# Weights loaded by halves of their columns, and a new order of the list of pieces, in a kernel of segmented attention beside a dense layer

## The chip, the core and the metric

The program runs on one core of one Trainium2 chip. The metric is device time in microseconds (us) of one execution; the time before is the median of three executions. TensorE is called PE here (its weight loads PEld), VectorE DVE, ScalarE ACT, GpSimd POOL, SyncE SP. SP computes nothing: its queue issues DMAs, in order.

## What is computed

A layer norm of `x` (2,048 rows of 512) feeds two branches, and their outputs are added to `x`:

```python
xn  = _layernorm(x)
out = x + _A_ref(xn, wq, wk, wv, wo, beta) + _B_ref(xn, w1, w2)
# A: 32 heads of width 16, the rows in 4 segments of 512
for s in range(4):
    p = softmax(q_s k_s^T * scale + causal mask)
    o = g * (phi(q_s) M) / (phi(q_s) z + 1e-6) + (1 - g) * (p v_s)   # g = sigmoid(beta)
    M = M + phi(k_s)^T v_s ;  z = z + sum(phi(k_s))                  # phi(t) = t+1 if t>0 else exp(t)
A = o @ wo
# B: dense layer of width 1,792
B = silu(xn @ w1) @ w2
```

All inputs and the output are bf16.

## The kernel before

The program is one long list of short words, `ORDER`, run from left to right; each word calls one helper (the table `PIECES`) that issues a handful of instructions. No scheduler moves them afterwards: on each engine, and on each engine's queue of DMAs, the instructions stand in the order in which the words stand. An engine whose next instruction waits holds up everything behind it on that engine. A word is a name and numbers: most often the segment first, then the block.

- `X t.n`, `XD t`: transposing normalized rows into `xnT`, on PE with a copy (`Xa`, `Xv`; L717, L720) for row tiles 0 to 3, by a transposing DMA on SP (L726) for tiles 4 to 15. `xs`, `xq`/`xi`/`xg`, `Nv`: statistics, root and normalization of a tile (DVE L270/L271 and L293, POOL L275/L278).
- `k s.i.part`, `q`, `v`, `h`: the projections. A block fills one PSUM bank of 512 columns in two parts of two matmuls (segment 0 of k, q, h: two parts of four matmuls of 256 columns). L314 and L325.
- A letter behind it evicts the bank: `kv`, `qv`, `vv` on DVE, `ka`, `qa`, `va` on ACT (L340, L350, L357). An eviction of k is followed by a masked copy `kTo` on POOL (L341). For h, `ha` is a tanh on ACT (L438) and `hv` the product on DVE (L443).
- `S t`: scores of one batch, t = 20 times the segment + 5 times the block of 8 heads + batch. PE fills `psS`, four banks, of which there is one copy (L642); one exponential over 2,048 columns on ACT writes `Pb` (L649); POOL masks the diagonal (L657). The next `S` can't start on PE before this exponential has read `psS`. There are 80 of them.
- `E n`, `O n`: products of the weights with v, even and odd heads (16 small matmuls, L676), evicted by `Ev`/`Ea`, `Ov`/`Oa` (L699, L706), after which SP moves rows (L691, L710).
- `fp`, `fa`, `fv` and `gp`, `ga`, `gv`: phi of k and of q on POOL, ACT (L374) and DVE (L384). `t`: phi(k) transposed by a DMA (L392). `m`, `mv`, `mw`: the memory M. `s`, `sv`, `r`, `w`, `d`, `z`, `R`, `W`: the divisors, their reciprocals (L491, L506) and their spreading by DMAs (L523). `n`, `nv`: phi(q) M and its addition (L549, L556). `dv`, `zv`: products with the spread factors (L545, L535).
- `o s.j.i`: one of 18 matmuls of the output tile j (14 with w2, 4 with wo; L595); `oh`, `sh` the same for the last tile by halves of its columns. `xl` loads x again for the residual (L562), `st` evicts an output tile on DVE and stores it (L569, L574), `sh` half a tile (L613, L617).
- `lw0`, `lw1`: loads of w2 and wo, issued on ACT's queue. `busy` is idle work on PE at the start.

The projections, `E`, `O`, `n` and the output tiles j = 0, 1 of the last segment (all tiles of the others) share four PSUM banks, the pool `pp` (tag `pb`): a block that opens a bank waits until one of the four has been evicted.

The loads at the start are issued on SP in this order: x tile 0, x tile 2 (tiles 1 and 3 on ACT's queue), wv in two halves of its rows, wk, wq, x tiles 4 to 7 (`x_hi`), w1, x tiles 8 to 11, x tiles 12 to 15, beta. All of them share the core's 16 DMA engines.

Of the kernel before, what the change touches and what calls it, by code (L numbers as in the profile page):

```python
# [13 lines left out]


ORDER = """
ones0 ones1 zeros xs0 xs1 xq0 xi0 busy44 xq1 Nv0 xi1 X0.1 Nv1 Xa0.1 busy6 X1.1 Xa1.1 v0.0.0 xs2 xs3 xq2 v0.0.1 xq3 xi2 va0.0 v0.1.0 Nv2 v0.1.1 va0.1 xi3 X2.1 Nv3 odd tb Xv2.1 k0.0.0 X3.1 Xv3.1 q0.0.0 q0.0.1 qv0.0 k0.0.1 xs7 xs4 ka0.0 k0.2.0 xs6 fp0.0
S0 v0.3.0 k0.1.0 k0.2.1 fa0.0 xs5 xg4.4 v0.3.1 kv0.2
S2 q0.1.0 k0.1.1 q0.1.1 vv0.3 fp0.2 v0.2.0 kv0.1 fa0.2 Nv7 Nv4
S1 qv0.1 v0.2.1 h0.10.0 h0.10.1 h0.7.0 xs8 vv0.2 ha0.10 h0.7.1 hv0.10 ha0.7  # L20
S4 Nv5 h0.4.0 h0.4.1 ha0.4 h0.11.0 hv0.7 k0.3.0 h0.11.1 ha0.11 xs9 hv0.11 fv0.2
S7 k0.3.1 q0.3.0 XD4 q0.3.1 hv0.4 q0.2.0 XD5 XD7 q0.2.1 fa0.1
S6 qv0.3 qv0.2 h0.13.0 h0.13.1 t0.2 v1.3.0 ha0.13 v1.1.0
S3 v1.1.1 kv0.3 Nv6 xs11 h0.5.0 hv0.13 h0.5.1 xs10 ha0.5 xg8.4 XD6 E0 vv1.1
S5 v1.3.1 lw0 hv0.5 vv1.3 k1.0.0 xs14 k1.2.0 k1.2.1
S9 h0.1.0 Ev0 Nv10 kv1.2 Nv9 h0.1.1 k1.0.1 E1 ha0.1
S13 kv1.0 h1.11.0 XD10 h0.2.0 h0.2.1 ha0.2 h1.11.1 Ev1 fv0.0 hv0.1
S8 hv0.2 tanh O0 h0.8.0 h0.8.1 bmask Ov0 q1.1.0 ha0.8 hv0.8
S12 q1.1.1 q1.3.0 q1.3.1 fa0.3 fp0.1 kind qv1.1 O1
S10 k1.3.0 k1.3.1 Ov1 XD9 q1.2.0 qv1.3 fp0.3 ha1.11 q1.2.1 Nv8  # L30
S11 kv1.3 h0.0.0 v1.0.0 v1.0.1 h0.0.1 Nv11 ha0.0
S16 qv1.2 vv1.0 h0.12.0 h0.12.1 fv0.3 fa1.0 k1.1.0 k1.1.1 fp1.0 hv0.0
S14 E2 hv1.11 h1.9.0 kv1.1 h1.9.1 ha0.12 Ev2 hv0.12
S15 fv0.1 v1.2.0 h0.6.0 xs15 h0.9.0 h0.6.1 ha0.6
S17 v1.2.1 t0.0 ha1.9 hv0.6 h0.9.1 vv1.2 q1.0.0 t0.3 q1.0.1
S19 t0.1 m0.2 qv1.0 hv1.9 gp1.1 mv0.2 ha0.9 fv1.0 XD8 XD11 E3 O2
S18 h0.3.0 h0.3.1 Ev3 xl0.2 m0.0 hv0.9 k2.2.0 Ov2 xs13 ha0.3 hv0.3
# [60 lines left out]
"""


# [1 line left out]
def kernel(  # L102
# [692 lines left out]
```

## Time and profile before

| what | us |
|---|---|
| median of three executions | 231.76 (231.45 to 232.0) |
| the profiled execution, its time | 231.23 |
| its span, from the first to the last instruction | 229.5 |
| PE busy, share of the span | 221.5, 97% |
| ACT busy | 198.9, 87% |
| DVE busy | 171.8, 75% |
| POOL busy | 114.8, 50% |

The span is 1.7 us shorter than the time of the same execution, which also holds what lies around the program. The granted clock of TensorE was 1.000 over the span. Busy times of PE are modelled from the starts of its matmuls and include their pipelined ends, so a busy PE can still have short pauses; the starts themselves are what is read below.

### The profile page before, as it was taken

What the parts mean: (1) busy time and instruction counts of PE and PEld (TensorE: products, weight loads), DVE (VectorE), ACT (ScalarE), POOL (GpSimd) and SP (SyncE); (2) the same over time, 40 slices, a digit from 0 to 9 for tenths busy, and PEclk for the clock granted to TensorE, in tenths of its full rate; (3) what the DMA queues carried; (4) which work ended last, traced back from release to release, by engine and by line L of the source; (5) the groups of instructions that cost most, each with busy time, mean ns of one, the idle gap of its engine ahead of it and who ended that gap; (6) DMA issues with size and microseconds to landing.
All of it is one profiled execution on the core that took longest, in us unless ns stands there. A gap on an engine that the chain in (4) does not pass through costs nothing.

```text
span 229.5 us, 5243 instructions
## 1 busy us (share of the span) xinstructions
PE 221.5 (97%) x1984; PEld 103.6 (45%) x1984; DVE 171.8 (75%) x349; ACT 198.9 (87%) x179; POOL 114.8 (50%) x173
## 2 busy tenths in 40 slices
PE   7899999989999999999999999999999999999993
PEld 7657645445533433333433433344433443434552
DVE  4699997978978758866596967845796868874744
ACT  3789999999999999999999999999999999996000
POOL 6068557576474586564574474655444473332000
PEclk9999999999999999999999999999999999999999
DMA  6993256014302424241115232203032111132132
GB/s 200 366 371 70 57 169 195 18 31 74 73 17 54 140 72 101 59 94 30 33 38 98 75 83 76 64 9 98 25 96 81 52 32 58 32 88 83 34 116 94
DMA packets 34778, 20.40 MB, mean 89 GB/s; under 512 B 15680, under 2 KB 34240, under 8 KB 34752
## 3 DMA queue, kind: packets, MB, share of 16 engines
q1 hardware_dynamic: 32128, 17.45, 27.6%
q10 hardware_dynamic: 2624, 2.62, 3.7%
q8 instruction: 15, 0.25, 0.5%
q14 instruction: 11, 0.09, 0.1%
HBM read 9.96 MB, written 2.10 MB: 53 GB/s over the span
## 4 chain that ended last, share of the span: by engine, by line
PE 77%; ACT 13%; DMA 3%; issue 2%; DVE 1%; SPq 1%; DVEq 0%; ACTq 0%
PE ps L314 26%; PE psO L595 25%; PE psS L642 10%; ACT Pb L649 10%; PE psV L676 8%; DMA wq_sb<-in_A_wq_dram 3%; PE psS L595 3%; PE ps L325 3%; ACT th L438 2%; PE ps L549 1%; ACT ex L374 1%; PE psM L400 1%; SPq L176 1%; DVE hT L443 1%; DVE o_out L569 1%
## 5 line engine op out<-in xcount | busy, mean ns | idle before, releaser
L649 ACT ACTIVATE Pb<-psS 128x2048 bf16<-128x2048 f32 x80 | 150.2, 1878 | 5.2 <-PE psS L642 4.0
L657 POOL TENSOR_SCALAR_AFFINE_SELECT Pb<-Pb 128x512 bf16<-128x512 bf16 (+1 forms) x112 | 81.2, 739 | 82.2 <-ACT Pb L649 81.8
L595 PE MATMUL psO<-w_sb,hT 128*128 128x512 bf16 x196 | 60.2, 381 | 0.0
L443 DVE SCALAR_TENSOR_TENSOR hT<-th,ps 128x512 bf16<-128x512 bf16 x56 | 37.8, 681 | 21.1 <-ACT th L438 20.9
L314 PE MATMUL ps<-xnT,w_sb 128*128 128x512 bf16 x168 | 45.5, 380 | 0.0
L595 PEld LDWEIGHTS <-hT 128*128 128x128 bf16 x238 | 22.0, 98 | 26.7 <-issue 6.6
L438 ACT ACTIVATE th<-ps 128x512 bf16<-128x512 f32 x56 | 32.6, 595 | 0.4 <-PE ps L314 0.4
L314 PEld LDWEIGHTS <-w_sb 128*128 128x128 bf16 x168 | 15.2, 98 | 18.0 <-issue 3.1
L676 PE MATMUL psV<-Pb,Vz 128*32 128x128 bf16 (+3 forms) x512 | 22.2, 301 | 0.0
L642 PE MATMUL psS<-qT,kT 16*128 16x256 bf16 (+3 forms) x256 | 17.3, 301 | 1.3 <-ACT Pb L649 0.3
L595 PE MATMUL psO<-wo_sb,oT 128*128 128x512 bf16 x56 | 18.2, 380 | 0.0
L314 PE MATMUL ps<-wv_sb,xnT 128*128 128x512 bf16 x64 | 18.0, 381 | 0.1
L642 PE MATMUL psS<-qT,kTo 32*128 32x384 bf16 (+3 forms) x256 | 17.2, 299 | 0.8 <-ACT Pb L649 0.2
L676 PEld LDWEIGHTS <-Vz 128*32 128x32 bf16 x512 | 11.0, 96 | 13.4 <-issue 5.5
L341 POOL TENSOR_SCALAR kTo<-kT,pm_odd 128x512 bf16<-128x512 bf16 x16 | 11.9, 745 | 10.2 <-ACT kT L340 8.2
L325 PE MATMUL ps<-xnT,w_sb 128*128 128x256 bf16 x112 | 14.6, 273 | 0.0
L706 DVE CAST odd<-psV 128x512 bf16<-128x512 f32 x15 | 10.3, 686 | 4.9 <-PE psV L676 4.8
L314 PE MATMUL ps<-xnT,wk_sb 128*128 128x512 bf16 x48 | 13.3, 380 | 0.1
L350 DVE CAST qT<-ps 128x512 bf16<-128x512 f32 x16 | 10.8, 680 | 3.5 <-PE ps L314 2.2
L642 PEld LDWEIGHTS <-kT 16*128 16x128 bf16 x256 | 5.8, 91 | 16.7 <-issue 15.5
L314 PE MATMUL ps<-xnT,wq_sb 128*128 128x512 bf16 x48 | 12.8, 380 | 0.0
L325 PEld LDWEIGHTS <-w_sb 128*128 128x128 bf16 x112 | 10.4, 98 | 3.9 <-issue 1.5
(95 smaller groups left out, 258.0 us busy)
## 6 DMA issues: line engine op xcount, KB each, us to landing
spr<-rz SPq DMA_DIRECT2D x56, 64.0 KB
x_res<-in_A_x_dram SPq DMA_DIRECT2D x16, 128.0 KB
out_dram<-o_out SPq DMA_DIRECT2D x15, 128.0 KB
w_sb<-in_B_w_dram SPq DMA_DIRECT2D x1, 1792.0 KB
w_sb<-in_B_w_dram ACTq DMA_DIRECT2D x1, 1792.0 KB
x_hi<-in_A_x_dram SPq DMA_DIRECT2D x2, 512.0 KB
oraw<-odd SPq DMA_DIRECT2D x64, 16.0 KB
wv_sb<-in_A_wv_dram SPq DMA_DIRECT2D x2, 256.0 KB
```

What stands on the lines that cost most here:

```text
L314: nc.tensor.matmul(sts[s][key][:, :], lhsT=lhsT(ki), rhs=rhs(ki), start=(ki == 0), stop=(ki == DT - 1))
L325: nc.tensor.matmul(sts[s][name, i][:, cols], lhsT=w_sb[:, ki, i * P : (i + 1) * P], rhs=xnT[:, ki, cols], start=(ki == 0), stop=(ki == DT ...
L341: nc.gpsimd.tensor_scalar(out=kTo[:, dt, :], in0=kT[:, dt, :], scalar1=pm_odd[:, 0:1], scalar2=1.0, op0=ALU.mult, op1=ALU.mult,)
L350: copy(out=seg_tile(s, "qT")[:, dt, :], in_=sts[s].pop(("q", dt))[:, :])
L438: nc.scalar.activation(out=th[:], in_=sts[s]["h", ft][:, :], func=AF.Tanh, scale=0.5)
L443: nc.vector.scalar_tensor_tensor(out=st["hT"][:, ft, :], in0=st.pop(("th", ft))[:], scalar=1.0, in1=st.pop(("h", ft))[:, :], op0=ALU.add, ...
L595: mm = nc.tensor.matmul(st["psO", *key], lhsT=lhsT, rhs=rhs, start=len(done) == 1, stop=len(done) == FT + DT)
L642: nc.tensor.matmul(psS[:, g, c0 : c0 + nq], lhsT=kk[rows, dt, kt * P : (kt + 1) * P], rhs=st["qT"][rows, dt, kt * P : L], start=True, stop ...
L649: exp = nc.scalar.activation(out=Pb[:, :, :], in_=psS[:, :, :], func=AF.Exp, scale=SCALE)
L657: mask = nc.gpsimd.affine_select(out=blocks, in_=blocks, compare_op=ALU.is_ge, fill=0.0, base=0, pattern=[[0, blocks.shape[1]], [1, P]], c ...
L676: nc.tensor.matmul(psV[32 * g : 32 * g + 32, kt * P : L], lhsT=Vzs[s % 2][:, kt, 4 * dt + g, par : par + 2, :].rearrange("p a d -> p (a d) ...
L706: copy(out=odd[:], in_=sts[s].pop(("psV", 1))[:, :])
```

## The change

Two things change. First, wk, wq and w1 are each loaded by two DMAs, the first half of the columns of wk and wq before the second halves. A row of wk or wq is 1,024 B in memory and each DMA now takes 512 B of it; of w1 1,792 B instead of 3,584 B:

```diff
-    def load_w(eng, w_sb, W, k0, k1):
-        eng.dma_start(out=w_sb[:, k0:k1, :], in_=W.rearrange("(ko ki) n -> ki ko n", ki=P)[:, k0:k1, :])
+    def load_w(eng, w_sb, W, k0, k1, cols=slice(None)):
+        eng.dma_start(out=w_sb[:, k0:k1, cols], in_=W.rearrange("(ko ki) n -> ki ko n", ki=P)[:, k0:k1, cols])
 
     load_w(nc.sync, wv_sb, A_wv, 0, 2)
     load_w(nc.sync, wv_sb, A_wv, 2, 4)
-    load_w(nc.sync, wk_sb, A_wk, 0, 4)
-    load_w(nc.sync, wq_sb, A_wq, 0, 4)
+    for cols in (slice(0, D // 2), slice(D // 2, D)):
+        load_w(nc.sync, wk_sb, A_wk, 0, DT, cols)
+        load_w(nc.sync, wq_sb, A_wq, 0, DT, cols)
     load_x(nc.sync, 4, 4)
-    load_w(nc.sync, w1_sb, B_w1, 0, DT)
+    for cols in (slice(0, F // 2), slice(F // 2, F)):
+        load_w(nc.sync, w1_sb, B_w1, 0, DT, cols)
     load_x(nc.sync, 8, 4)
     load_x(nc.sync, 12, 4)
```

Second, `ORDER` is another order of the same 1,147 words, apart from seven evictions that change engine: `va0.2`, `qa3.2` and `Oa14` go from DVE to ACT, `vv3.3`, `kv3.0`, `Ev9` and `Ev15` from ACT to DVE. The new order came out of the same planning as the old one, with longer transposing transfers, last evictions and last stores assumed in it; the helpers are unchanged. Shown are its start and its last steps, and of the new list two steps between them:

```diff
-ones0 ones1 zeros xs0 xs1 xq0 xi0 busy44 xq1 Nv0 xi1 X0.1 Nv1 Xa0.1 busy6 X1.1 Xa1.1 v0.0.0 xs2 xs3 xq2 v0.0.1 xq3 xi2 va0.0 v0.1.0 Nv2 v0.1.1 va0.1 xi3 X2.1 Nv3 odd tb Xv2.1 k0.0.0 X3.1 Xv3.1 q0.0.0 q0.0.1 qv0.0 k0.0.1 xs7 xs4 ka0.0 k0.2.0 xs6 fp0.0
-S0 v0.3.0 k0.1.0 k0.2.1 fa0.0 xs5 xg4.4 v0.3.1 kv0.2
-S2 q0.1.0 k0.1.1 q0.1.1 vv0.3 fp0.2 v0.2.0 kv0.1 fa0.2 Nv7 Nv4
-S1 qv0.1 v0.2.1 h0.10.0 h0.10.1 h0.7.0 xs8 vv0.2 ha0.10 h0.7.1 hv0.10 ha0.7
-S4 Nv5 h0.4.0 h0.4.1 ha0.4 h0.11.0 hv0.7 k0.3.0 h0.11.1 ha0.11 xs9 hv0.11 fv0.2
-S7 k0.3.1 q0.3.0 XD4 q0.3.1 hv0.4 q0.2.0 XD5 XD7 q0.2.1 fa0.1
-S6 qv0.3 qv0.2 h0.13.0 h0.13.1 t0.2 v1.3.0 ha0.13 v1.1.0
-S3 v1.1.1 kv0.3 Nv6 xs11 h0.5.0 hv0.13 h0.5.1 xs10 ha0.5 xg8.4 XD6 E0 vv1.1
-S5 v1.3.1 lw0 hv0.5 vv1.3 k1.0.0 xs14 k1.2.0 k1.2.1
-S9 h0.1.0 Ev0 Nv10 kv1.2 Nv9 h0.1.1 k1.0.1 E1 ha0.1
-S13 kv1.0 h1.11.0 XD10 h0.2.0 h0.2.1 ha0.2 h1.11.1 Ev1 fv0.0 hv0.1
-S8 hv0.2 tanh O0 h0.8.0 h0.8.1 bmask Ov0 q1.1.0 ha0.8 hv0.8
-S12 q1.1.1 q1.3.0 q1.3.1 fa0.3 fp0.1 kind qv1.1 O1
-S10 k1.3.0 k1.3.1 Ov1 XD9 q1.2.0 qv1.3 fp0.3 ha1.11 q1.2.1 Nv8
...
-S79 w3 h3.13.0 h3.13.1 ha3.13 hv3.11 o2.1.15 xl2.1 o2.1.1 h3.6.0 h3.10.0 hv3.13 d3.3 o2.1.0
-S78 o2.1.14 h3.10.1 R0.3 h3.9.0 h3.6.1 R0.1 o2.1.13 d3.0 o2.1.11 R0.0 o2.1.6 R0.2 W0 ha3.10
-S76 o2.1.9 hv3.10 ha3.6 o2.1.3 d3.1 o2.1.8 h3.9.1 o3.1.0 o3.1.2 dv3.0 o3.1.13 ha3.9 dv3.3 o3.1.8 o3.1.4 oh3.1 oh12.1 o3.2.12 z3.2 z3.0 o3.1.11 o3.2.2 oh0.0 hv3.6 hv3.9 d3.2 o3.2.0 E15 Ea15 O15 o3.1.1 o3.2.13 zv3.0 o3.1.5 o3.2.3 Oa15 o2.1.10 dv3.2 o3.0.12 o3.0.5 o3.2.5 z3.1 xl3.1 n3.0 xl3.3 o3.0.6 nv3.0 zv3.2 o3.2.9 o3.0.0 o3.2.6 o3.0.4 o3.2.4 o2.1.12 n3.2 o2.1.5 oh2.0 oh14.1 oh2.1 oh12.0 o3.2.1 o3.2.14 dv3.1 oh6.1 oh5.1 nv3.2 o3.1.16 o3.0.11 o3.1.9 oh8.1 R1.1 o3.0.3 oh5.0 oh10.1 R1.3 oh6.0 oh10.0 o2.1.2 oh7.0 o3.0.10 oh13.1 o3.0.2 R1.0 oh9.0 R1.2 o3.1.12 n3.1 oh14.0 W1 z3.3 o3.2.10 o3.0.1 o3.2.11 o3.1.7 oh11.1 o3.2.7 o3.1.14 zv3.1 nv3.1 o3.0.9 o3.0.13 st2.1 o3.2.8 oh15.0 n3.3 zv3.3 oh16.0 oh8.0 oh3.0 o3.0.15 o3.0.14 o3.0.16 oh1.0 o3.0.7 o3.2.16 nv3.3 oh11.0 o3.2.17 o3.2.15 xl3.2 o3.1.6 o3.0.8 oh4.0 oh17.0 st3.2 o3.1.10 oh13.0 o3.0.17 o3.1.15 o3.1.17 o3.1.3 sh0 oh16.1 oh9.1 st3.0 oh4.1 st3.1 oh1.1 oh15.1 oh0.1 oh17.1 oh7.1 sh1
+ones0 ones1 zeros xs0 xs1 xq0 xi0 busy44 xq1 Nv0 xi1 X0.1 Nv1 Xa0.1 busy6 X1.1 Xa1.1 v0.0.0 xs2 xs3 xq2 v0.0.1 xq3 xi2 va0.0 v0.1.0 Nv2 v0.1.1 va0.1 xi3 X2.1 Nv3 odd tb Xv2.1 k0.0.0 X3.1 Xv3.1 q0.0.0 q0.0.1 qv0.0 k0.0.1 v0.2.0 xs6 xs4 k0.1.0 xs5 xs7 ka0.0 fa0.0
+S0 q0.1.0 k0.2.0 v0.2.1 xg4.4 va0.2 k0.2.1 fp0.0
+S2 k0.1.1 kv0.2 k0.3.0 k0.3.1 fa0.2 kv0.1 kv0.3 Nv5 q0.1.1
+S4 v0.3.0 XD5 v0.3.1 h0.7.0 h0.7.1 ha0.7 fv0.0
+S1 Nv7 qv0.1 h0.13.0 h0.13.1 Nv4 h0.11.0 Nv6 h0.11.1 hv0.7 fp0.2 ha0.13 fp0.1 vv0.3 q0.3.0 ha0.11 XD7
+S6 q0.3.1 h0.4.0 xs13 h0.4.1 tanh hv0.13 qv0.3 hv0.11 XD4 ha0.4 v1.3.0 xs9 xs11 hv0.4 h0.5.0 xs10
+S7 v1.3.1 h0.5.1 vv1.3 q0.2.0 fa0.1 XD6 q0.2.1
+S5 E0 qv0.2 ha0.5 Ev0 h0.10.0 xs8 h0.10.1 fv0.1 v1.1.0 ha0.10 hv0.10
+S16 v1.1.1 h0.1.0 h0.1.1 ha0.1 E1 vv1.1 fp0.3
+S3 q1.1.0 fv0.2 xg8.4 hv0.5 q1.1.1 h0.8.0 Ev1 h0.8.1 ha0.8
+S9 xs14 k1.2.0 k1.2.1 qv1.1 hv0.8 h0.2.0 fa0.3 t0.0 O0 t0.1
+S8 kind kv1.2 h0.2.1 k1.1.0 Ov0 ha0.2 k1.0.0 k1.0.1 Nv10 hv0.1 Nv11
+S14 hv0.2 XD10 h1.11.0 Nv8 k1.1.1 h1.11.1 ha1.11 Nv9 kv1.1 XD8 k1.3.0
+S11 XD11 k1.3.1 v1.0.0 kv1.0 lw0 kv1.3 hv1.11 v1.0.1 vv1.0 h0.12.0
+S12 O1 h0.9.0 h0.12.1 q1.0.0 Ov1 ha0.12
+S10 fp1.0 q1.3.0 fv0.3 h0.9.1 hv0.12 ha0.9 q1.0.1 h0.6.0 qv1.0 t0.3
+S15 v1.2.0 q1.3.1 h0.6.1 hv0.9 h0.3.0 ha0.6
+S13 qv1.3 E2 hv0.6 XD9 h0.3.1 t0.2 bmask h0.0.0 Ev2 ha0.3 v1.2.1
+S19 h0.0.1 gate ha0.0 vv1.2 k2.1.0 hv0.3 k2.1.1 O2
...
+S20 v2.1.0 xs12 v2.1.1 hv1.8 sv0 o0.0.0 o0.0.12 r0.3 vv2.1 xl0.2 h1.4.0 ha1.0 o0.0.3
+S23 h1.4.1 h1.10.0 r0.0 o0.0.13 h1.10.1 ha1.4 r0.2 o0.0.2 r0.1 o0.0.7 hv1.0 ha1.10 w0 z0.3 o0.0.5 gp1.3 z0.2 gp1.2 hv1.10
...
+S77 h3.10.1 st2.2 ha3.10 hv3.5 o2.1.11 h3.7.0 r3.0 w3 h3.6.0 h3.6.1 R0.2 hv3.10 R0.0 o2.1.15 o2.1.2 xl3.0 R0.3 o2.1.1 h3.7.1 ha3.6 hv3.6 o2.1.10 d3.0 o2.1.0 ha3.7
+S79 R0.1 o3.0.1 W0 o3.0.5 o3.0.10 d3.1 o2.1.17 o2.1.16 h3.11.0 o3.0.6 h3.11.1 o3.0.12 ha3.11 o3.0.3 hv3.7 o3.0.2 hv3.11 o2.1.9 dv3.1 o3.0.8 dv3.0 d3.2
+S78 z3.1 E15 h3.9.0 z3.0 o3.0.0 o2.1.7 h3.9.1 ha3.9 o2.1.12 z3.2 oh11.1 oh7.0 Ev15 dv3.2 oh1.0 oh7.1 o2.1.5 hv3.9 o3.2.1 o3.2.6 o2.1.3 O15 Oa15 zv3.1 o2.1.13 n3.1 o3.2.13 nv3.1 zv3.2 oh2.1 zv3.0 o3.2.7 n3.2 o3.2.8 o3.0.13 o3.0.11 o3.2.4 nv3.2 oh12.1 oh15.0 o3.0.9 o2.1.8 n3.0 R1.3 o3.1.5 nv3.0 o3.0.16 oh3.0 o3.1.7 o3.1.3 o3.1.8 R1.1 R1.0 d3.3 oh10.1 o3.2.16 o3.1.16 oh15.1 oh9.1 o3.2.9 oh4.0 o3.2.5 oh0.0 o3.2.3 oh4.1 R1.2 o3.2.15 o3.1.11 oh0.1 oh14.0 oh13.0 oh1.1 W1 oh16.0 z3.3 oh10.0 o3.1.13 o3.0.7 dv3.3 o3.0.14 o3.2.2 o3.1.1 o3.2.12 oh11.0 o3.2.11 oh13.1 oh6.0 oh12.0 oh2.0 o3.0.4 oh5.0 n3.3 o3.2.14 st2.1 zv3.3 oh8.1 o3.2.0 o3.1.14 oh3.1 nv3.3 o3.1.12 o3.0.15 o3.1.4 o3.0.17 o3.2.10 oh17.0 oh16.1 o3.2.17 o3.1.10 oh6.1 xl3.3 o3.1.2 o3.1.6 oh17.1 xl3.1 oh5.1 st3.0 oh14.1 oh8.0 oh9.0 st3.2 o3.1.15 sh0 sh1 o3.1.9 o3.1.0 o3.1.17 st3.1
```

In the words of the list, what changes by place: in front of S0 stand `v0.2.0`, `k0.1.0` and `fa0.0` in the new list and `k0.2.0` and `fp0.0` in the old one. The load of w2 (`lw0`) stands in the step of the 13th score batch (S11) instead of the 8th (S5). The last score batch is S78 instead of S76, with `E15` right behind it; the list ends with the store of a whole tile (`st3.1`) instead of half a tile (`sh1`).

## The prediction, made before the changed kernel had run

> **What bounds it now.** I read the page first, then the chain of waits in order of time, then the timeline of the start and of the end. Of the page:
>
> ```profile
> PE 221.5 (97%) x1984; PEld 103.6 (45%) x1984; DVE 171.8 (75%) x349; ACT 198.9 (87%) x179; POOL 114.8 (50%) x173
> ...
> PE   7899999989999999999999999999999999999993
> ...
> ACT  3789999999999999999999999999999999996000
> ```
>
> PE and ACT are both full from slice 3 on, and ACT runs out three slices before PE: the end is set by PE, its work plus its pauses. The chain gives the prices of PE's words:
>
> ```profile
> 203.09 0.33 PE psS L642 x4
> ...
> 205.03 0.65 PE psO L595 x3
> ```
>
> An S is 0.33, an output product 0.22, so a part of a projection (two such matmuls) 0.43; an E or O, in another line of the chain, 0.66. Now the timeline of the start:
>
> ```profile
> 10.25 0.77 PEld L325 LDWEIGHTS <-wq_sb 128*128 128x128 bf16 x8 [0.82 <-DMA wq_sb<-in_A_wq_dram]
> ...
> 11.77 0.59 ACT L340 CAST kT<-ps 128x512 bf16<-128x512 f32 x1 [0.91 <-PE ps L325]
> 11.95 0.69 DVE L270 BATCH_NORM_STATS2 stats<-x_hi 128x6 f32<-128x512 bf16 x1
> ...
> 12.41 0.39 PE L642 MATMUL psS<-qT,kT 16*128 16x512 bf16 x4 [0.24 <-ACT kT L340]
> ...
> 12.86 1.88 ACT L649 ACTIVATE Pb<-psS 128x2048 bf16<-128x2048 f32 x1 [0.50 <-PE psS L642]
> ...
> 15.24 1.88 ACT L649 ACTIVATE Pb<-psS 128x2048 bf16<-128x2048 f32 x1
> ...
> 17.61 1.88 ACT L649 ACTIVATE Pb<-psS 128x2048 bf16<-128x2048 f32 x1
> ...
> 20.38 1.87 ACT L649 ACTIVATE Pb<-psS 128x2048 bf16<-128x2048 f32 x1
> ```
>
> The reader is to see two things. From one exponential to the next are 2.38 us (12.86, 15.24): 1.88, then 0.50 until the next scores are there, in which one short activation fits; with two tanhs between them it is 2.77 (17.61, 20.38). And the row of 10.25 names what S0 hangs on, below. With the prices I add PE's words between two S and hold them against the starts of the S on PE (first at 12.41, last, S76, at 205.61: 79 steps in 193.20). A step takes the larger of 2.38 and its PE words plus 0.11 (steps of 2.48 take 2.59 or 2.60). Counted off the old list: 60 steps with up to 2.28 of PE words, 16 with 2.48 to 2.50, 3 with 2.70: 60 x 2.38 + 16 x 2.60 + 3 x 2.81 = 192.8, 0.4 under the measured time. So the old list ran nearly without waits that its words don't explain, and four terms make the span: 12.41 to S0; 193.20 of steps; from S76 to PE's end 20.39 (20.00 of words, 0.23 of waits, 0.16 for the last matmul to drain; end at 226.0); and the tail, 3.51.
>
> **The start, before S0.** PE waits for wq until 10.25, and the eviction of k, S0 and the first exponential hang on that. By the trace's landing events wk is complete at 8.35, wq at 10.21, x_hi at 11.69, w1 at 16.41, one after another: the loads are bound by the DMA engines. A packet of 1,024 B from memory takes 46 ns, one of 3,584 B 144; packets of 512 B appear only from on-chip memory (27 ns), those of 256 B take 18. I take 27. A half of wk is 32 packets on each of 16 engines, 32 x 27 = 0.86 us (bounds: 0.58 at 18, 1.47 at 46). The first halves of wk and wq then land 1.7 us behind wv (6.96), with the spread of the engines near 9.0 (8.1 to 9.9). The next limit is the copy of x tile 3, done at 10.06: `q0.0.0` follows `X3.1` at 9.44, `q0.0.1` starts at 10.17, then `k0.0.1` (to 11.05), `v0.2.0` and `k0.1.0` (to 11.92), while ACT evicts k from 11.25 to 11.84. S0 at 11.95: **-0.46** (0 if wq still came at 10.2). `v0.2.0` is 0.43 of PE work that S0 no longer has behind it; it shows in the last term. `fa0.0` falls into the 0.50 in which ACT waits for S0: free.
>
> **Behind the loads.** All packets of wk and wq cost 128 x 27 instead of 64 x 46 ns: x_hi at 11.69 + 0.51 = 12.20 (bounds: 11.05 at 18 ns, 14.63 at 46). w1 by 1,792 B, between 46 and 144 ns, 75 on the line through both: 64 x 75 against 32 x 144, +0.2, so w1 at about 17.1; its first reader `h0.7.0` comes near 18.0. Three more issues on SP of some 0.5 us, ahead of a transposing DMA that comes only at 18: free. But the four statistics of x_hi now head DVE's queue, and behind them stand `kv0.2`, `kv0.1`, `kv0.3`, whose PSUM banks PE wants back. At 0.80 a statistic and 0.60 an eviction (three in a row start at 15.15, 15.72 and 16.32 in the timeline) DVE is done with `kv0.2` at 16.05 (`v0.3.0` wants its bank at 17.1), `hv0.7` at 20.9 (`q0.3.0`: 21.2), `hv0.4` at 26.3 (E0: 27.05), `vv1.3` at 27.7 (`h0.10.0`: 27.7), `hv0.10` at 30.95 (E1: 30.8, but the S behind it can't start before 31.9). I take no stall; the cover is 0 to 1 us thick, and what DVE loses beyond it PE loses too.
>
> **The steps.** Counted off the new list: 68 steps up to 2.29, 8 with 2.48 to 2.50, and 2.71, 3.56, 3.78 once each: 68 x 2.38 + 8 x 2.60 + 2.82 + 3.67 + 3.89 = 193.0. The same 0.4 that the count missed before makes 193.4. Added: steps with two tanhs. In S5 PE has only 2.28: +0.39 less slack, 0.36; S23 (2.48), +0.16; S0 with `va0.2` (0.64 on ACT) +0.07, S7 +0.06. The other four doubles lie in or before longer PE steps: nothing. Sum **194.0** (193.4 without these).
>
> **Moved DMAs.** w2 is now loaded from about 42 to 49 us. The one transposing DMA under the old load of w2 (issued 34.47) landed after 4.0 us, others after 2.4 to 2.5. Under it or just behind now come `O1`'s row moves, `t0.3` and XD9 on SP: six issues of 0.5 to 0.6, two of 1.2, XD9 landing near 53.1; `k2.1.0` reads it at 54.1. Free by 1.0; with 1.5 us more it costs 0.5. The seven evictions that change engine are one more for DVE, one less for ACT, inside steps with room; free, else 0.6 once.
>
> **The end.** From S78 PE has 18.48 of words, against 20.00; with the same 0.39, **18.87**. The late chain there is `O15`, ACT's copy, the row moves (1.55 from issue to landing), the `R1`, the spread (2.1), `zv3.3`, `nv3.3`. Before, `nv3.3` ended 11.6 after O15 on PE and its first reader came 11.9 after it; now, with SP free of the first two row moves, I get 10.4 against a reader at 11.0. Free, by 0.6. The tail before:
>
> ```profile
> 226.11 0.41 DVE L613 SCALAR_TENSOR_TENSOR o_half<-psS,x_res 128x256 bf16<-128x256 f32 x1
> ...
> 227.06 0.40 SPq L617 DMA_DIRECT2D out_dram<-o_half  x1
> ```
>
> The half tile was evicted by 226.52, but SP was issuing other stores until 226.97; it landed 1.61 after its issue. Now a whole tile comes last: eviction to 0.8 after PE's end, SP free, landing 1.84 to 1.90: 2.7 in all, as before (2.67). Tail **3.5**.
>
> **Sum.** 11.95 + 194.0 + 18.87 + 3.5 = 228.3 against 229.5: -1.2. The profiled execution took 231.23, 0.53 under the median shown: 230.0 in its frame, **230.6** against the median of 231.76.
>
> **Rivals.**
> 1. *No room lost* (231.76 - 1.85 = 229.9): the doubled tanhs hide in slack that I don't see. For: the old S1, S4 and S77, each with two, cost nothing beyond PE's words. Against: S5 has few of these. 0.12.
> 2. *The halves don't bring wq earlier*, because one slow engine sets the landing (12 of 16 engines had wq by 9.2, the last at 10.21). S0 stays at 12.41: 230.6 + 0.46 = 231.0. 0.08.
> 3. *DVE's queue eats it*: each eviction counts its full 0.68 instead of 0.60. Fourteen of them stand up to `hv0.10`: 32.05 instead of 30.95, so E1 ends at 32.75 and S3 comes 0.85 late: 231.4. For: bank by bank the cover is thin. Against: three evictions in a row in the old run kept 0.60. Within 0.2%. 0.18.
> 4. *Slower: x_hi is late.* If a 512 B packet from memory costs what one of 1,024 B does, x_hi lands at 14.63 and all that DVE does until `Ev1` shifts by 2.4 us, PE with it by about 2.2: 232.8. It decides from a stall of about 1.2, x_hi at 13.5 (37 ns a packet). Against: 27 ns in this trace; for: not one of these came from memory. 0.15.
>
> The Trainium skill, page "DMA: Bandwidth & Descriptors", section "Bandwidth", speaks for rival 4: it wants DMAs batched to 1 MiB and gives 2.0 us plus the bytes at 436 GB/s for each. By that, an estimate, four loads of 256 KB one behind the other take 10.4 us instead of 6.4, and x_hi would be 4 us late. The trace disagrees so far: whole wk and wq landed 1.4 and 1.9 us behind their forerunners, so loads in one queue overlap their fixed parts.
>
> **Chances and range.** Forecast 0.47, rivals 0.12, 0.08, 0.18, 0.15. About 0.2% (0.46 us) can be told from no change: faster (under 231.3) is the forecast and rivals 1 and 2, 0.67; same rival 3, 0.18; slower rival 4, 0.15. The forecast's own range is 230.0 to 231.2, by the stalls taken as nothing and the double tanhs; the range of 8 in 10 goes down past rival 1 and up through rival 3 to the near part of rival 4: 229.5 to 232.4.
>
> **What would show it.** Right: no wait for wq at the first q, S0 at 11.9 to 12.0, x_hi's first statistic near 12.2, S78 near 206, O15's reader of `nv3.3` unstopped, a tail of 3.5. Wrong: a first statistic after 13, PE waiting for DVE's evictions between 17 and 33 us, a pause before `k2.1.0`, or steps of 2.27 that take more than 2.4.

## The result, and the profile after

| | median, us | range | runs |
|---|---|---|---|
| kernel before, same chip | 232.12 | 231.45 to 232.75 | 6 |
| changed kernel | 237.91 | 236.48 to 239.2 | 6 |

The ratio is 1.0254, with a 95% interval from 1.0213 to 1.0295: the changed kernel is slower by 2.5%, where 230.6 us and a small gain were forecast. The profiled execution took 237.82 us, its span 236.1, against 228.3 in the prediction's sum. Of the page after:

```profile
PE 223.9 (95%) x1984; PEld 103.6 (44%) x1984; DVE 173.7 (74%) x350; ACT 198.9 (84%) x178; POOL 114.7 (49%) x173
...
PE   7998999995999999999899999999999999999992
...
PEclk9999999999799999999999999999999999999999
```

The loss is local. PE's row has one slice at 5, the tenth (53 to 59 us), and the clock that PE was granted has one slice below 9, the eleventh. PE's work is the same, so a longer span means pauses. The start, by contrast, came out as forecast; in the timeline of the start:

```profile
11.81 0.69 DVE L272 BATCH_NORM_STATS2 stats<-x_hi 128x6 f32<-128x512 bf16 x1 [0.36 <-DMA x_hi<-in_A_x_dram]
...
11.95 0.39 PE L644 MATMUL psS<-qT,kT 16*128 16x512 bf16 x4
```

S0 starts at 11.95, and x_hi's first statistic at 11.81, 0.14 ahead of the old run. (Lines of the code stand two further down than before.) The waits of PE between 11 and 230 us are few. Before:

```profile
PE psS L642 <- ACT Pb L649: 0.6, 2, 0.3
PE psS L642 <- ACT kT L340: 0.2, 1, 0.2
```

and after (us in total, times, the longest):

```profile
PE ps L316 <- DMA xnT<-xn_t: 2.7, 1, 2.7
PE psM L402 <- DMA phiK<-pk: 0.9, 1, 0.9
PE ps L327 <- DMA xnT<-xn_t: 0.7, 1, 0.7
```

Three single waits replace the short ones for ACT. The longest, in the timeline of PE:

```profile
54.17 0.40 PE L644 MATMUL psS<-qT,kTo 32*128 32x384 bf16 x8
54.50 0.61 PE L327 MATMUL ps<-xnT,w_sb 128*128 128x256 bf16 x4
57.82 1.02 PE L316 MATMUL ps<-xnT,wk_sb 128*128 128x512 bf16 x4 [2.71 <-DMA xnT<-xn_t]
...
61.11 1.06 PE L402 MATMUL psM<-Vz,phiK 128*128 128x128 bf16 x8
```

The 57.82 row is `k2.1.0` in S19, which reads what XD9 transposes. Its cause lies 15 us earlier, in the timeline of SP's queue:

```profile
42.73 4.29 SPq L728 DMA_TRANSPOSE xnT<-xn_t  x3
47.12 1.14 SPq L693 DMA_DIRECT2D zraw<-odd  x2
48.31 4.66 SPq L712 DMA_DIRECT2D oraw<-odd  x4
53.08 2.05 SPq L394 DMA_TRANSPOSE phiK<-pk  x1
55.17 1.26 SPq L728 DMA_TRANSPOSE xnT<-xn_t  x1
```

The three transposes at 42.73 are XD10, XD8 and XD11. The load of w2 was issued on ACT's queue at 42.71. By the landing events it lasted until 52.4, and the three landed 6.8, 8.4 and 7.3 us after their issue, instead of 2.4 to 2.5. Nobody on PE waits for them yet; SP does. In the view of SP's waits between 40 and 60 us the fourth row move of O1 stands behind one of them:

```profile
SPq L712 <- DMA xnT<-xn_t: 2.3, 1, 2.3
```

That move left at 52.46, t0.3 at 53.08 (its issue alone took 2.05 us instead of 1.2), XD9 at 55.17 (my estimate was 50.7). The trace says why a row move waits for a transpose of other data. Each DMA of this program reports its landing on a semaphore, a counter; there are eight of them for all DMAs, on SP's queue and on ACT's, used nearly in turn, and in none of the twelve traces does a DMA leave before the one that used its semaphore last has landed. The move of 52.46 has the semaphore of XD8 (landed 52.45), t0.3 that of XD11 (52.98), and XD9 that of the load of w2 itself (52.44): XD9 could not have left before that, however fast the transposes. XD9 itself was quick, issued 55.17 and landed at 57.69: it was sent late, not carried slowly. And PE did not come back at full speed; the windows of the same stretch (busy time of each engine, granted clock, DMA share, GB/s):

```profile
56.00:58.00 2.00, 0.18 (x1) 0.13 (x2) 0.00 (x0) 0.99 (x2) 1.23 (x2) 1.00 0.45 92
...
59.00:60.00 1.00, 1.00 (x24) 0.42 (x16) 0.15 (x1) 0.00 (x0) 0.00 (x0) 0.53 0.02 4
60.00:61.00 1.00, 1.00 (x10) 0.28 (x3) 1.00 (x2) 0.60 (x1) 0.00 (x0) 0.50 0.55 131
61.00:62.00 1.00, 1.00 (x10) 0.89 (x9) 0.13 (x1) 1.00 (x1) 0.00 (x0) 0.50 0.01 2
62.00:63.00 1.00, 1.00 (x11) 0.61 (x10) 0.79 (x2) 0.80 (x2) 0.65 (x1) 0.77 0.03 6
```

The granted clock is 0.50 for 3.41 us after the pause: the eight matmuls of M at 61.11 take 1.06 instead of 0.61. (In two of the six executions, 236.48 and 237.87 us, the mean granted clock was 0.998 and 1.000, and such a stretch alone takes off 0.007: there it was missing.) Held against the prediction's rule (the larger of 2.38 and the PE words plus 0.11), the steps around it are too long by 3.18 (S19), 1.08 (S17) and 0.14 (S18): 4.4 us of the 7.8 by which the span was missed. The rest is in smaller pieces: S1 0.83, S42 1.12, S28 0.52, the last stretch 0.33, the tail 0.63.

S1, in the timeline of DVE:

```profile
17.16 1.58 DVE L386 SCALAR_TENSOR_TENSOR pk<-ex,pos 128x512 bf16<-128x512 bf16 x1
...
19.96 1.49 DVE L295 TENSOR_SCALAR xn_t<-x_hi,mv_all,rstd_all 128x512 bf16<-128x512 bf16 x2
21.37 0.67 DVE L445 SCALAR_TENSOR_TENSOR hT<-th,ps 128x512 bf16<-128x512 bf16 x1
```

`fv0.0` takes 1.58 and the two normalizations 1.49, where elsewhere such an instruction takes 0.68 and 0.40. So `hv0.7` (21.37) ends at 22.04 instead of the 20.9 that I had worked out, and `q0.3.0` starts at 22.09; the profile puts that wait down to a transposing DMA (XD7), which landed at 22.11, behind that start, and whose rows `q0.3.0` does not read. S42, in the chain of waits:

```profile
113.02 3.92 DMA phiK<-pk
```

`m1.0` waited for t1.1's transpose, which landed 3.92 us after its issue at 113.02. At 114.52 a load of instructions (16,384 B, 0.88 us) ran on the same DMA engines. The tail, in the timeline of DVE:

```profile
231.14 0.69 DVE L571 SCALAR_TENSOR_TENSOR o_out<-psS,x_res 128x512 bf16<-128x512 f32 x1 [1.26 <-PE psS L597]
...
232.41 0.68 DVE L571 SCALAR_TENSOR_TENSOR o_out<-psO,x_res 128x512 bf16<-128x512 f32 x1
```

PE ended at 231.96, but `st3.1`, the last eviction, stood behind `st3.2` and two half tiles and started at 232.41.

### The profile page after: what moved, and what is told of

Same layout as the page of the kernel before. It is cut to its first block, busy times and chain, and to the rows that moved or that the text cites. A ratio compares the mean times of both kernels' runs of the same rounds, so it can differ in the third digit from the quotient of the medians.

```text
span 236.1 us, 5232 instructions
## 1 busy us (share of the span) xinstructions
PE 223.9 (95%) x1984; PEld 103.6 (44%) x1984; DVE 173.7 (74%) x350; ACT 198.9 (84%) x178; POOL 114.7 (49%) x173
## 4 chain that ended last, share of the span: by engine, by line
PE 67%; DVE 11%; DMA 8%; issue 5%; ACT 4%; SPq 4%; DVEq 0%
PE ps L316 23%; PE psO L597 21%; PE psS L644 8%; PE psV L678 7%; DMA spr<-rz 3%; DMA x_hi<-in_A_x_dram 3%; PE psS L597 2%; ACT Pb L651 2%; DVE stats L272 2%; PE ps L327 2%; DVE hT L445 2%; DMA phiK<-pk 2%; ACT th L440 2%; SPq L176 1%; PE psM L402 1%
## 5 line engine op out<-in xcount | busy, mean ns | idle before, releaser
L659 POOL TENSOR_SCALAR_AFFINE_SELECT Pb<-Pb 128x512 bf16<-128x512 bf16 (+1 forms) x112 | 79.5, 724 | 90.4 <-ACT Pb L651 88.2
L597 PE MATMUL psO<-w_sb,hT 128*128 128x512 bf16 x196 | 63.1, 380 | 0.3 <-DVE oT L558 0.2
L316 PE MATMUL ps<-xnT,w_sb 128*128 128x512 bf16 x168 | 46.5, 380 | 0.0
L678 PE MATMUL psV<-Pb,Vz 128*32 128x384 bf16 (+3 forms) x512 | 23.2, 305 | 0.0
L597 PE MATMUL psO<-wo_sb,oT 128*128 128x512 bf16 x56 | 20.2, 381 | 0.0
L644 PE MATMUL psS<-qT,kT 16*128 16x128 bf16 (+3 forms) x256 | 17.4, 303 | 0.8
L708 DVE CAST odd<-psV 128x512 bf16<-128x512 f32 x14 | 9.7, 690 | 11.0 <-PE psV L678 11.0
L343 POOL TENSOR_SCALAR kTo<-kT,pm_odd 128x512 bf16<-128x512 bf16 x16 | 12.8, 803 | 8.6 <-ACT kT L342 7.6
L316 PE MATMUL ps<-xnT,wq_sb 128*128 128x512 bf16 x48 | 14.2, 396 | 0.0
L352 DVE CAST qT<-ps 128x512 bf16<-128x512 f32 x15 | 10.2, 683 | 4.0 <-PE ps L316 3.3
```

The lines of the kernel that those rows point to most:

```text
L316: nc.tensor.matmul(sts[s][key][:, :], lhsT=lhsT(ki), rhs=rhs(ki), start=(ki == 0), stop=(ki == DT - 1))
L343: nc.gpsimd.tensor_scalar(out=kTo[:, dt, :], in0=kT[:, dt, :], scalar1=pm_odd[:, 0:1], scalar2=1.0, op0=ALU.mult, op1=ALU.mult,)
L352: copy(out=seg_tile(s, "qT")[:, dt, :], in_=sts[s].pop(("q", dt))[:, :])
L597: mm = nc.tensor.matmul(st["psO", *key], lhsT=lhsT, rhs=rhs, start=len(done) == 1, stop=len(done) == FT + DT)
L644: nc.tensor.matmul(psS[:, g, c0 : c0 + nq], lhsT=kk[rows, dt, kt * P : (kt + 1) * P], rhs=st["qT"][rows, dt, kt * P : L], start=True, stop ...
L659: mask = nc.gpsimd.affine_select(out=blocks, in_=blocks, compare_op=ALU.is_ge, fill=0.0, base=0, pattern=[[0, blocks.shape[1]], [1, P]], c ...
```

## Experiments

All ratios are against the kernel before on the same chip. Its medians there were 231.53 for the first four kernels, 231.91 for the next four and 232.03 for the last two. In the edits below, a line of the list is shown as far as its words matter; its rest is left out.

| label | what | ratio (95%) |
|---|---|---|
| w2_early | new list, w2 loaded as early as before | 1.0129 (1.0071 to 1.0187) |
| old_list_halves | old list, halves | 1.0005 (0.9976 to 1.0035) |
| new_list_whole | new list, whole loads | 1.0172 (1.0103 to 1.0242) |
| fill_the_wait | changed kernel, PE kept busy in the pause | 1.0120 (1.0063 to 1.0176) |
| t03_behind | w2_early, t0.3 behind XD9 | 1.0082 (1.0057 to 1.0106) |
| nv_behind | and two normalizations later in S1 | 1.0105 (1.0077 to 1.0133) |
| tail_early | and st3.2 earlier | 1.0151 (1.0126 to 1.0176) |
| old_list_w2_late | old list, w2 loaded later | 1.0212 (1.0173 to 1.0251) |
| halves_nv_behind | old_list_halves, two normalizations later | 0.9992 (0.9967 to 1.0016) |
| old_nv_behind | the same move alone | 1.0001 (0.9974 to 1.0027) |

**Which half of the change.** In old_list_halves the old list stays and the loads are those of the changed kernel; in new_list_whole it is the other way round.

> The old list with the loads of wk, wq and w1 by halves of their columns. Theory (the halves do what they say and nothing else): the first q does not wait for wq, S0 starts at 11.9 to 12.0 instead of 12.41, the steps are those of the kernel before; 0.45 us less, 231.6 to 231.8 us, ratio 0.998. Rival (the halves themselves cost something: x_hi or w1 late): S0 as early, but a wait for x_hi or w1 between 12 and 25 us, and a ratio of 1.000 or above.

> The new list with the loads of wk, wq and w1 whole again. Theory (the order of the list alone makes the loss): q waits for wq until 10.2, S0 at 12.4 to 12.5, the pause in S19 is there as before; 0.45 us more than the changed kernel, 238.3 us, ratio to the kernel before 1.027. Rival (the halves have a part in the loss): less than the changed kernel, under 237.5.

Whole loads under the new list cost 1.7% (k2.1.0 late again, behind a pause of 1.89 us, granted clock 0.50 for 3.41 us from 57.1); halves under the old list cost and bring nothing that ten runs tell. So the list is the cause of most of the loss. But 1.027 was a miss, and 236.33 us is under the 237.5 that the rival named: whether the halves have a part in the 0.8% between 1.0172 and 1.0254 is not shown. The two intervals overlap, and the stretch at half clock came less often here (in three of the four executions the mean clock was 0.996 or more). S0 came at 12.05, not at 12.4 to 12.5, because wq had landed at 9.55. In old_list_halves S0 started at 12.07 (12.41 before), but S4 then became 0.65 longer. In its timeline of PE:

```profile
21.17 0.60 PE L327 MATMUL ps<-xnT,w_sb 128*128 128x256 bf16 x4 [0.33 <-DVE Vz L359]
```

The bank of `vv0.2` is waited for, and DVE had reached it late, behind statistics that began 0.45 later (x_hi landed at 12.38) and behind two normalizations of 1.75 us (1.03 before).

**The load of w2.** The word that loads w2 back at the head of S5:

```diff
-S5 E0 qv0.2 ha0.5
+S5 lw0 E0 qv0.2 ha0.5
...
-S11 XD11 k1.3.1 v1.0.0 kv1.0 lw0 kv1.3
+S11 XD11 k1.3.1 v1.0.0 kv1.0 kv1.3
```

> The new list with one word moved: the load of w2 (lw0) stands at the head of step S5 instead of inside S11, so it runs from about 28 to 36 us, where the new list has no transposing DMA of x. Theory (three transposing DMAs and the row moves shared the DMA engines with the load of w2, so XD9 was issued and landed late): k2.1.0 in S19 waits at most 0.3 us instead of 2.9, TensorE has no pause, its clock stays at 1.000, steps S19, S17 and S18 take 2.4 to 2.5 each; 4.4 us less, about 233.5 us, still 0.5% over the kernel before. Rival (XD9 is late because it stands behind O1's moves and t0.3 in SP's queue, whatever else is loaded): k2.1.0 still waits 2 us or more, 236.5 to 238. Rival (the contention only moves): t0.0, t0.1 or E0's row moves land 4 to 8 us after their issue and a step before S12 grows by more than 1 us.

Half of the loss went with this one word. w2 was loaded from 28.3 to 36.7, XD10, XD8 and XD11 landed after 2.4 to 2.5 us, SP's queue ran through, and the clock stayed at 1.00. In SP's timeline:

```profile
42.98 3.82 SPq L728 DMA_TRANSPOSE xnT<-xn_t  x3
46.90 1.14 SPq L693 DMA_DIRECT2D zraw<-odd  x2
48.10 2.45 SPq L712 DMA_DIRECT2D oraw<-odd  x4
50.65 1.22 SPq L394 DMA_TRANSPOSE phiK<-pk  x1
51.91 1.26 SPq L728 DMA_TRANSPOSE xnT<-xn_t  x1
```

Four row moves take 2.45 instead of 4.66. XD9 goes out 3.3 us earlier, but lands 4.08 after its issue (a load of instructions ran from 53.06 for 1.39 us), and k2.1.0 still starts 0.95 late.

**The same in the other list.** The prediction that a transpose under the load of w2 is slow should hold in any list. In the old one the load alone was moved:

```diff
-S5 v1.3.1 lw0 hv0.5 vv1.3
+S5 v1.3.1 hv0.5 vv1.3
...
-S17 v1.2.1 t0.0 ha1.9
+S17 lw0 v1.2.1 t0.0 ha1.9
```

> The old list with whole loads, where only the load of w2 is moved, from S5 to the head of S17, so that XD8 and XD11 (which the old list issues in S19) come under it. Theory (a): a transposing transfer under the load of w2 lands after 6 to 8 us instead of 2.5, in any list: k2.2.0 in S18 waits 1.5 to 4 us, TensorE's granted clock falls to 0.5 for some 3.4 us if the pause is 2.5 us or longer; 1.5 to 5 us slower, ratio 1.007 to 1.02. Rival (b): what was slow in the new list is its crowd of transfers (row moves and three transposes within 3 us), not the load: XD8 and XD11 land after 2.5 to 4 us, ratio 1.000.

One word makes the old kernel 2.1% slower. Four transposes fell under the load (issued 53.70 to 58.15) and landed after 6.3, 7.8, 6.6 and 5.7 us. What stopped PE was not `k2.2.0` in S18, as expected, but a transpose of phi(k), read by M in S19. The chain of waits there:

```profile
53.70 6.34 DMA phiK<-pk
60.04 0.05 issue
60.09 0.61 PE psM L400 x4
```

and the windows of the stretch:

```profile
58.00:60.00 2.00, 0.00 (x0) 0.00 (x0) 0.00 (x0) 0.60 (x2) 1.67 (x3) 0.67 1.12 343
60.00:62.00 2.00, 1.91 (x24) 1.06 (x28) 1.16 (x5) 0.00 (x0) 0.17 (x1) 0.50 1.16 330
62.00:64.00 2.00, 2.00 (x23) 0.86 (x16) 2.00 (x4) 0.46 (x1) 0.00 (x0) 0.50 0.75 123
```

PE paused for 3.56 us, and the granted clock fell to 0.50 for 6.83 us. The DMA engines are full at 330 to 343 GB/s: w2's 1,792 KB fill them, and the transposes, 128 KB each, have to share them. Rival (b) of the expectation, the crowd of other transfers, falls: SP issued nothing but four transposes in this stretch. The Trainium skill, page "DMA: Bandwidth & Descriptors", section "Queues, rings and completion order", says that each DMA engine alternates between its queues a packet at a time, and drains a whole packet of one queue before it goes to the next. That fits transfers that come through slowly while the load lasts. In the packet records of the changed kernel 281 packets of SP's queue (the transposes' are of 256 B) and 285 of the load (1,024 B) went through between 47 and 48 us, which agrees; between 44 and 46 us only the load's did, though XD10 had been issued at 42.73, and no run here shows why. By the landing events they come through near the load's end: at 60.0, 63.0, 63.4 and 63.9 with the load done at 63.2 here, at 49.6, 52.4 and 53.0 with the load done at 52.4 in the changed kernel.

**The pause and the clock.** In the changed kernel, 26 small matmuls of the identity with itself, into a bank that nobody reads, in front of k2.1.0:

```diff
-S19 h0.0.1 gate ha0.0 vv1.2 k2.1.0
+S19 h0.0.1 gate ha0.0 vv1.2 fw26 k2.1.0
...
+    def fill_wait(n):
+        ps = bank([P, L], F32, "ps")
+        for i in range(n):
+            nc.tensor.matmul(ps[:, 0:P], lhsT=ident[:], rhs=ident[:], start=True, stop=True)
```

> The changed kernel with 26 matmuls of the identity with itself (106 ns each, 2.8 us) into a PSUM bank that nobody reads, put between h0.0.1 and k2.1.0, where TensorE waited 2.9 us. They change no value of the output. Theory (the clock of 0.50 for 3.4 us behind the pause is the answer to the pause): the granted clock stays at 1.000 there, S17 takes 2.4 instead of 3.46 and S18 2.4 instead of 2.52, k2.1.0 starts when XD9 has landed as before; 1.3 us less, about 236.6. Rival (the drop of the clock has another cause): it comes at the same place, 237.9 or more.

In its timeline of PE:

```profile
54.94 1.61 PE L741 MATMUL ps<-ident 128*128 128x128 bf16 x26
57.18 1.02 PE L316 MATMUL ps<-xnT,wk_sb 128*128 128x512 bf16 x4 [0.63 <-DMA xnT<-xn_t]
```

The 26 took 1.61 us, not 2.8, so a pause of 0.63 was left. XD9 was still late (issued 54.52, landed 57.05), yet the clock stayed at 1.00 and S17 and S18 had their normal length: 1.2 us, as expected. The run gained more than that, 1.3%. In the profiled execution XD9 was also issued 0.65 earlier, S42 was 1.1 shorter and S41 0.3 longer, which the added matmuls don't explain.

**What is left in S19.** On w2_early, t0.3 moved from the end of S10 to behind XD9:

```diff
-S10 fp1.0 q1.3.0 fv0.3 h0.9.1 hv0.12 ha0.9 q1.0.1 h0.6.0 qv1.0 t0.3
+S10 fp1.0 q1.3.0 fv0.3 h0.9.1 hv0.12 ha0.9 q1.0.1 h0.6.0 qv1.0
...
-S13 qv1.3 E2 hv0.6 XD9 h0.3.1
+S13 qv1.3 E2 hv0.6 XD9 t0.3 h0.3.1
```

> The new list with the load of w2 at the head of S5 (the run before it with that edit alone: 1.013 of the kernel before, k2.1.0 in S19 0.95 us late, XD9 issued at 51.91 and landed 4.08 us later) and, besides, t0.3 moved behind XD9 on SP. Theory (a): what is left in S19 is XD9's place in SP's queue behind t0.3 (1.2 us of issue): XD9 issued near 50.7, S19's wait gone, 0.9 us less, ratio about 1.009. Rival (b): the rest of the wait is the slow landing alone, whatever the place: XD9 lands after 4 us again and half of the 0.95 stays. Rival (c): t0.3, now later, is itself waited for by m0.2, and the 0.9 comes back in S17 or S18: ratio 1.013.

Theory (a): in the timeline of PE the pause is gone,

```profile
54.73 0.61 PE L327 MATMUL ps<-xnT,w_sb 128*128 128x256 bf16 x4
55.17 1.03 PE L316 MATMUL ps<-xnT,wk_sb 128*128 128x512 bf16 x4
```

S19 and S17 have no excess, and the ratio of 1.008 is near the 1.009 expected. The load of instructions now met t0.3, which landed after 4.12 us and was not waited for.

**The smaller pieces.** On t03_behind, two normalizations moved on DVE; and on that, st3.2 moved in the last step:

```diff
-S1 Nv7 qv0.1 h0.13.0 h0.13.1 Nv4 h0.11.0 Nv6 h0.11.1 hv0.7 fp0.2 ha0.13 fp0.1 vv0.3 q0.3.0
+S1 Nv7 qv0.1 h0.13.0 h0.13.1 h0.11.0 h0.11.1 hv0.7 fp0.2 ha0.13 fp0.1 vv0.3 Nv4 Nv6 q0.3.0
...
-o3.2.17 o3.1.10 oh6.1 xl3.3 o3.1.2 o3.1.6 oh17.1 xl3.1 oh5.1 st3.0 oh14.1 oh8.0 oh9.0 st3.2 o3.1.15
+o3.2.17 st3.2 o3.1.10 oh6.1 xl3.3 o3.1.2 o3.1.6 oh17.1 xl3.1 oh5.1 st3.0 oh14.1 oh8.0 oh9.0 o3.1.15
```

> The same, and in S1 the two normalizations Nv4 and Nv6 moved on DVE behind vv0.3, so that hv0.7 comes some 1.5 us earlier. Theory (a): S1's 0.8 us is the wait of q0.3.0 for the bank that hv0.7 empties, and DVE has room behind it: S1's excess goes to nearly 0, ratio about 0.0035 lower than in the run with t0.3 alone (1.0055). Rival (b): DVE as a whole has no room there, and the 0.8 appears again at the next evictions (S6, S7, S5) or as a late transpose of tiles 4 to 7: same ratio.

> The same, and in the last step st3.2 moved from behind oh9.0 to right behind o3.2.17, the last product of its tile. Theory (a): the tail of 4.1 to 4.6 us is st3.2's eviction, which waits for every product written to the shared banks before it in the list, and st3.1 queued behind it on DVE: tail 3.5 to 3.8, ratio 0.003 lower again, about 1.002. Rival (b): the tail is st3.1's own eviction and landing, and st3.2's place changes nothing: ratio as in the run before. All three together leave the new list near the kernel before; nothing in them makes it clearly faster.

Both are misses. In nv_behind S1's excess is gone and S6, the next step, has 0.85: rival (b), DVE as a whole has no room there. In its profiled execution S36 and S43 were also late by 1.2 each. S36, in the timeline of DVE:

```profile
98.24 0.56 DVE L295 TENSOR_SCALAR xn_t<-x_end,mv_all,rstd_all 128x512 bf16<-128x512 bf16 x1 [1.88 <-DMA xnT<-xn_t]
98.72 0.67 DVE L445 SCALAR_TENSOR_TENSOR hT<-th,ps 128x512 bf16<-128x512 bf16 x1
```

A normalization waits for XD13 to be done with its buffer, and an eviction of h that PE needs stands behind it. XD13 landed after 4.53 us, with a load of instructions from 95.37 (1.13 us). In tail_early the tail grew to 5.4 us. In the timeline of DVE:

```profile
228.79 0.76 DVE L615 SCALAR_TENSOR_TENSOR o_half<-psS,x_res 128x256 bf16<-128x256 f32 x2 [2.05 <-DMA x_res<-in_A_x_dram]
```

The store of st3.2 now stood on SP ahead of the loads of x for the last tiles, and SP waited with it for the eviction. The tail was not cured; that st3.2's place costs 0.6 in the changed kernel remains read from its trace only.

**Can the halves be kept?** The old list with halves, and Nv7 and Nv4 behind vv0.2; and the same move with whole loads:

```diff
-S2 q0.1.0 k0.1.1 q0.1.1 vv0.3 fp0.2 v0.2.0 kv0.1 fa0.2 Nv7 Nv4
-S1 qv0.1 v0.2.1 h0.10.0 h0.10.1 h0.7.0 xs8 vv0.2 ha0.10
+S2 q0.1.0 k0.1.1 q0.1.1 vv0.3 fp0.2 v0.2.0 kv0.1 fa0.2
+S1 qv0.1 v0.2.1 h0.10.0 h0.10.1 h0.7.0 vv0.2 Nv7 Nv4 xs8 ha0.10
```

> The old list with wk, wq and w1 by halves, and the two normalizations Nv7 and Nv4 moved on DVE from the end of S2 to behind vv0.2 in S1. In the run of the halves alone (ratio 1.0005) S0 came 0.35 us earlier and k0.3.0 in S4 waited 0.65 us for a bank that vv0.2 empties, behind two normalizations of 1.75 us on DVE. Theory (a): that wait took the gain; without it the halves are worth 0.3 to 0.7 us, ratio 0.997 to 0.999. Rival (b): DVE as a whole is late by x_hi's later landing, and hv0.10 or hv0.7 now holds up a bank: ratio 1.000 to 1.003.

> The same move of Nv7 and Nv4 alone, with the old list and whole loads: there vv0.2 is waited for by nobody, so both theories say no gain, ratio 1.000 (to 1.002 where the later normalizations make XD4 and XD7 or hv0.10 late).

S4's wait is gone with the halves and S0 stays at 12.09 (x_hi had also landed 0.86 earlier in this execution than in that of old_list_halves, so the move alone is not shown to have cured it). But the intervals of both hold 1.000: a gain of 0.3 us, if there is one, is below what twelve runs tell. No version was measured to beat the kernel before.

## Why the prediction was wrong

**The step that failed: "Moved DMAs".** It saw the right thing and applied it to the wrong transfers. It read that the one transpose under the old load of w2 had landed after 4.0 us, and put the new load at 42 to 49 us (it ran from 42.7 to 52.4). But it then named as coming "under it or just behind" only O1's row moves, t0.3 and XD9. XD10, XD8 and XD11 stand in S14 and S11 of the new list, beside the load, and are missing. So XD9's issue was worked out as six issues of 0.5 to 0.6 and two of 1.2 in a free queue, with a row move held up by nothing. "Free by 1.0; with 1.5 us more it costs 0.5" became 3.18 of pause and 1.22 of half clock. It also mis-sized the price. In the old trace the load of w2 ran from 30.28 to 37.99, and the transpose issued at 34.47 landed at 38.47: it had met only the last 3.5 us of the load. The transposes issued nearer to the load's start, in the changed kernel and in old_list_w2_late, took 5.7 to 8.4 us. And XD9's issue could not have been at 50.7 with the load in flight until 52.44, whose semaphore it shares. No rival held this case, though a pause before `k2.1.0` stands among the signs of being wrong.

**The start was right, to the hundredth by luck.** The first q waits for wq no longer, and S0 is at 11.95. But S0 scatters: it starts at 11.89 to 12.22 in the eight traces with halves, and at 12.05 to 13.63 in the four with whole loads, where wq lands at 9.55 to 11.42. The gain of 0.46 is that of one pair of executions. x_hi came at 11.78, not 12.20. The 512 B packets from memory took 27 ns in the median, as taken, and wq came 3.45 us behind wv, as in the sum (128 x 27 ns). Mis-sized were the whole loads: wq 3.25 us behind wv, not 64 x 46 ns = 2.94. So rival 4 is out, and with it the estimate beside it: the four loads of 256 KB landed 0.8 to 0.9 us apart. (The Trainium skill, page "DMA: Bandwidth & Descriptors", has that sum in its section "Anatomy of one DMA — SWDGE (gpsimd) path", for DMAs issued from GpSimd; these were issued on SP.) The sum also carried the gain at S0 through to the end; in the trace of old_list_halves S4 gave it back.

**DVE's cover.** "I take no stall; the cover is 0 to 1 us thick" cost 0.83 in S1. Rival 3 named the queue and the place, with too small a reason (0.68 instead of 0.60 for an eviction): evictions kept their time, and it was instructions with all operands in SBUF that took about twice as long. nv_behind shows that DVE has no slack there to shift this to.

**The steps.** Apart from the stalls the count held: of 200.82 measured against 194.0, the excesses of S19, S17, S18, S1, S42 and S28 make 6.87. That the rest meets 194.0 is partly luck: of the four steps made longer for their two tanhs, S5 took 0.26 over the rule (0.36 was taken) and S0, S7 and S23 nothing. Neither S42 (1.12) nor S28 (0.52) was in the sum. S42 is a transpose that landed 1.4 late beside a load of instructions. The old trace has such loads too: a transpose issued at 121.82 landed after 3.94 us with one at 122.92. The prediction did not reckon with them. In S28 a spreading transfer (issued at 77.25) landed after 4.51 us, against 2.11 in the last step. It stands beside the load of wo (512 KB, issued at 77.37, landed at 81.56), the same kind of neighbour as in S19. The old trace has this too: one issued at 73.51, 0.28 behind the load of wo, landed after 4.14. No run moved that load.

**The end.** The last stretch took 19.20 instead of 18.87, the tail 4.13 instead of "3.5". "2.7 in all" was right for the eviction and the landing of one whole tile; the term left out the evictions that stand ahead of it on DVE.

**What stays open.** With w2 early and t0.3 moved the new list is still 0.8% slower. S1, S36 and the tail hold most of it in that trace (0.88 and 1.16 of excess, a tail of 4.13 instead of 3.51). S36 and S42 change from one kernel to the next, as the place of the instruction loads does, and how much of the 0.8% these are was not separated.

## What to carry to other kernels

When a large load is moved in time, list every transfer that will be in flight beside it, on all queues, and let each land when the load ends, not after its usual time; then follow the queue that issues them, because a late completion there holds up transfers that are themselves fast, here through the semaphore that they share. A pause of PE costs more than its own length where the granted clock drops behind it. And a gain at the start counts only when the next queue on its way, here DVE's, has room for it.

## What the runs showed of the hardware

- A transpose by DMA landed 2.4 to 2.5 us after its issue when alone, and after 5.7 to 8.4 us under the load of 1,792 KB of w2, in two lists. The load itself took 7.7 us in the kernel before, with one transpose beside it, 8.4 in w2_early, with no XD in flight, 9.3 with four transposes, and 8.9 to 9.7 with three (three traces).
- A single pause of PE of 2.71 us was followed by 3.41 us at a granted clock of 0.50, one of 1.89 us (new_list_whole) by as much, one of 3.56 us by 6.83, one of 0.79 us (w2_early) by none. With matmuls in all but 0.63 us of the wait it stayed at 1.00. The drop did not come in every execution: of the six of the changed kernel two were without it.
- Instruction loads of 16,384 B come every 10 to 17 us and took 0.9 to 1.7 us. Transposes that landed after 3.9 to 4.5 us (behind the start, and without w2) all had one in flight beside them; no run moved these loads alone.
- DVE was slow beside POOL. The normalizations of x_hi took 0.396 and 0.400 us where POOL was idle, and 0.447 to 0.851 where it was busy throughout. The evictions of h, which read PSUM, took 0.68 beside an idle POOL and 0.69 beside a busy one, in the median. The Trainium skill, page "SBUF — State Buffer", section "Who interferes with whom", gives the two engines one shared pair of SBUF ports, which one instruction at a time holds to its end; the trace agrees in which instructions suffer, but not each of them does: phi took 1.58 us at 17.16, and 0.68 to 0.74 at 46.35, 88.08 and 127.84 beside a POOL as busy. No run here took POOL's work away.
